# Gated attention and channel mix on one core: state products between half-chunks accumulated in the output's PSUM bank, merged scans, and the low parts of four weights formed by TensorE

## The chip, the cores and the metric

The kernel runs on one core of a Trainium2 chip. The metric is device time in microseconds (us) of one execution. The median of three runs of the kernel before is 344.0 us (342.59 to 344.41).

## What is computed

For 4 batches, 8 heads, 768 positions and a head size of 48, a gated linear attention runs over the positions; its output, 384 features for each position, goes through a channel mix with a shift by one position, 1024 hidden features and a sigmoid gate. All is float32.

```python
for t in range(S):
    state = alpha[:, :, t, :, None] * state + einsum('bhd,bhe->bhde', k[:, :, t], v[:, :, t])
    y[:, :, t] = einsum('bhd,bhde->bhe', q[:, :, t], state)
# x = y, heads joined to 384 features; x_prev = x shifted by one position
xk = mu_k * x + (1 - mu_k) * x_prev
xr = mu_r * x + (1 - mu_r) * x_prev
k = maximum(xk @ w_k, 0)
out = sigmoid(xr @ w_r) * ((k * k) @ w_v)
```

## The kernel before

**Attention.** The sequence of each batch is cut into three segments of 256 positions (12 segments, numbered `a`), each of two chunks of 128 positions (24 chunks, numbered `i`), each of two half-chunks of 64. For a segment, VectorE (DVE) runs scans over `alpha`: `forth` (L380) makes running products, three scans of 256 columns, one for each feature tile; `turn` (L417) takes reciprocals of their last columns; `back` (L424) makes the products from the other end, three scans of 255 columns. `times` (L408) multiplies q and k by them. GpSimd (POOL) copies end values aside (`ends`, L396 and L398), and transfers move the rows of the fourth head pair (`gather`, L446).

For a chunk, TensorE (PE) transposes k (`trans`, L483), ScalarE (ACT) copies that out (`keep`, L661). `update` (L500) multiplies k and v into the state's growth of both half-chunks; it lies in the PSUM tile `yu` beside the output. `scores` (L512) multiplies k and q into the PSUM tile `sp`; DVE applies the mask (`masked`, L597) and adds the growth to the state (`advance`, L628, L631, at a segment's end L633). `intra` (L528) multiplies masked scores and v into `yu`; `inter(i, 0)` (L550) adds the products of q with the state to `yu`, for the heads whose rows of the array go with that bank; `inter(i, 1)` makes the products for the other half, which would be written from rows 0 to 63 into the bank of rows 64 to 127 and the other way round, and writes them into free columns of `sp`. ACT copies the output from `yu` (`leave`, L575), and `crossed` (L585) adds the products in `sp` to it, two DVE additions for a chunk. `spread` (L594) moves rows of the output by two transfers and `prefix` (L568, L570) on POOL fills the column of the position before; then the segment is ready for the channel mix.

An attention step on PE is either an `enter` (update and scores of one chunk), a `visit` (intra and inter of one chunk) or, from chunk 4 on (`JOINED`), a visit that also enters the next chunk.

**Channel mix.** The segments go through in seven groups, the first two of one segment (256 columns), the others of two (512 columns). Products are made in three terms, high by high, low by high and high by low part: `mix_ops` blends x (L802, L805) and splits it (L808, L811); `up_ops` (L822 to L837) makes eight tiles of 128 hidden features, squares and splits them; `gate_ops` (L847, L852) makes the gate; `down_ops` (L859) the output, closed by DVE (L981) and stored (L986). The three PSUM tiles `pm` are taken in turn.

**Weights.** They come in ten blocks (`wk` 4, `wr` 2, `wv` 4), through two raw buffers (`RAWS`): load (L751), `head_bits` on ACT (L756), `join` on DVE (L764), the high part on ACT (L772), the low part on DVE by a subtraction (L776). A raw buffer is free for the next block when its low part is made.

**Order.** All jobs are put into a plan with the engine and what each needs. The list `ORDER` fixes the order on each engine; `follow` only sorts the issue across engines by planned start. Each engine's queue, POOL's and SP's (transfers) among them, then runs in order. Ahead of the first channel-mix products, while PE has gaps, zero matmuls fill them (L1074), until the third user of the `pm` tiles has started (`filled`).

Of the kernel before, what the change touches and what calls it, by code (L numbers as in the profile page):

```python
# [33 lines left out]
LMAX = 2 * C  # L34
WMAX = 2 * LMAX
# [17 lines left out]
ISSUE = 0.42  # L53
RAWS = 2
# [11 lines left out]
class Plan:  # L66
# [26 lines left out]
    def rings(self, sizes):  # L93
        for (ring, n), writers in self.first.items():
            for old in self.users.get((ring, n - sizes[ring]), ()):
                for w in writers:
                    if old != w:
                        self.need[w].append(old)
# [15 lines left out]

    def follow(self, sizes, order):

        self.rings(sizes)
        pre, suc = self.links()
        n = len(self.eng)
# [91 lines left out]
def gated_attention_channel_mix(  # L211
# [64 lines left out]
    for t in (none, *rings):  # L276
        POOL.memset(t, 0.0)  # L277
# [979 lines left out]
```

## Time and profile before

| what | value |
|---|---|
| median of three runs | 344.0 us |
| profiled execution, its own time | 343.89 us |
| its span in the trace | 342.2 us |
| PE busy | 325.7 us, 95% of the span |
| DVE busy | 220.4 us, 64% |
| ACT busy | 196.2 us, 57% |
| POOL busy | 17.9 us, 5% |

The profile is of one execution; its own time is 1.7 us more than the span from the first to the last instruction. Busy shares are averages over the whole span; the stretches differ, which the rows below show.

### The profile page before, as it was taken

What the parts mean: (1) busy time and instruction counts of PE and PEld (TensorE: products, weight loads), DVE (VectorE), ACT (ScalarE), POOL (GpSimd) and SP (SyncE); (2) the same over time, 40 slices, a digit from 0 to 9 for tenths busy, and PEclk for the clock granted to TensorE, in tenths of its full rate; (3) what the DMA queues carried; (4) which work ended last, traced back from release to release, by engine and by line L of the source; (5) the groups of instructions that cost most, each with busy time, mean ns of one, the idle gap of its engine ahead of it and who ended that gap; (6) DMA issues with size and microseconds to landing.
All of it is one profiled execution on the core that took longest, in us unless ns stands there. A gap on an engine that the chain in (4) does not pass through costs nothing. (4 is left out here: it accounts for less than half of the span.)

```text
span 342.2 us, 10261 instructions
## 1 busy us (share of the span) xinstructions
PE 325.7 (95%) x4421; PEld 278.7 (81%) x4421; DVE 220.4 (64%) x421; ACT 196.2 (57%) x367; POOL 17.9 (5%) x60
## 2 busy tenths in 40 slices
PE   8868896999999999999999999999999999999992
PEld 8757885999998888888888888888788887888781
DVE  5999998879988949427564896264895112943010
ACT  4548896476664959137742399622498521887100
POOL 7202001000101000000000000000000000000000
PEclk9999999699999999999999999999999999999997
DMA  7988865443453442211163440043510001100011
GB/s 266 326 284 264 284 198 161 121 125 87 119 165 99 96 119 65 79 20 40 18 200 101 150 129 8 2 119 92 149 35 10 0 15 44 61 2 1 1 63 36
DMA packets 17204, 35.54 MB, mean 104 GB/s; under 512 B 3584, under 2 KB 7808, under 8 KB 17152
## 3 DMA queue, kind: packets, MB, share of 16 engines
q1 hardware_dynamic: 17008, 34.81, 34.0%
q8 instruction: 36, 0.59, 0.7%
q14 instruction: 16, 0.13, 0.1%
q10 hardware_dynamic: 144, 0.00, 0.0%
HBM read 26.55 MB, written 4.72 MB: 91 GB/s over the span
## 5 line engine op out<-in xcount | busy, mean ns | idle before, releaser
L822 PE MATMUL pm<-xkh,wkh 128*128 128x512 f32 (+1 forms) x168 | 44.0, 369 | 0.9 <-ACT x L802 0.9
L828 ACT ACTIVATE r<-pm 128x512 f32<-128x512 f32 (+1 forms) x56 | 29.7, 534 | 22.0 <-PE pm L822 21.5
L822 PE MATMUL pm<-xkh,wkl 128*128 128x512 f32 (+1 forms) x168 | 42.2, 359 | 0.0
L822 PE MATMUL pm<-xkl,wkh 128*128 128x512 f32 (+1 forms) x168 | 42.2, 359 | 0.0
L859 PE MATMUL pm<-kha,wvh 128*128 128x512 f32 (+1 forms) x108 | 39.4, 365 | 2.3 <-ACT wvh L772 2.3
L859 PE MATMUL pm<-kb,wvh 128*128 128x512 f32 x120 | 41.3, 401 | 0.0
L859 PE MATMUL pm<-kha,wvl 128*128 128x512 f32 (+1 forms) x108 | 38.3, 355 | 0.7 <-DVE wvl L776 0.7
L859 PE MATMUL pm<-kla,wvh 128*128 128x512 f32 (+1 forms) x108 | 38.2, 353 | 0.0
L822 PEld LDWEIGHTS pm<-xkh,wkl 128*128 128x128 f32 x168 | 29.3, 188 | 6.0 <-issue 1.0
L981 DVE TENSOR_TENSOR sig<-pm,sig 128x512 f32<-128x512 f32 (+1 forms) x21 | 12.7, 611 | 32.1 <-PE pm L859 23.6
L822 PEld LDWEIGHTS pm<-xkl,wkh 128*128 128x128 f32 x168 | 29.3, 188 | 4.9
L802 ACT ACTIVATE x<-xt,mu 128x512 f32<-128x512 f32 (+1 forms) x42 | 25.5, 656 | 12.3 <-DMA xt<-xt 12.1
L822 PEld LDWEIGHTS pm<-xkh,wkh 128*128 128x128 f32 x168 | 28.6, 188 | 4.9
L834 ACT ACTIVATE k<-r 128x512 f32<-128x512 f32 (+1 forms) x56 | 31.5, 565 | 1.0 <-DVE kla L837 0.5
L575 ACT COPY xt<-yu 112x512 f32<-112x512 f32 x24 | 14.0, 584 | 26.6 <-PE yu L550 23.5
L837 DVE TENSOR_TENSOR kb<-k,kb 128x512 fp32r<-128x512 f32 x20 | 13.8, 690 | 20.9 <-ACT k L834 13.8
L805 DVE SCALAR_TENSOR_TENSOR x<-xt,nu,x 128x512 f32<-128x512 f32 (+1 forms) x42 | 27.0, 668 | 0.3 <-ACT x L802 0.3
L859 PEld LDWEIGHTS pm<-kb,wvh 128*128 128x128 f32 x120 | 22.6, 188 | 5.1
L661 ACT COPY ht<-pt 128x384 f32<-128x384 f32 x24 | 16.2, 677 | 16.4 <-PE pt L483 16.3
L859 PEld LDWEIGHTS pm<-kha,wvh 128*128 128x128 f32 x108 | 21.6, 200 | 5.0 <-ACT wvh L772 2.5
L837 DVE TENSOR_TENSOR kla<-k,kha 128x512 fp32r<-128x512 f32 (+1 forms) x36 | 20.0, 566 | 8.3 <-ACT k L834 4.1
L380 DVE TENSOR_TENSOR_SCAN pp<-al,tiny 128x256 f32<-128x256 f32 x36 | 23.5, 679 | 2.4 <-POOL st L277 2.4
(90 smaller groups left out, 614.2 us busy)
## 6 DMA issues: line engine op xcount, KB each, us to landing
v<-v_p SPq DMA_DIRECT2D x12, 400.0 KB, 4.1
al<-al_p SPq DMA_DIRECT2D x12, 384.0 KB, 3.4
q<-q_p SPq DMA_DIRECT2D x12, 384.0 KB, 3.7
k<-k_p SPq DMA_DIRECT2D x12, 384.0 KB, 3.9
out<-sig SPq DMA_DIRECT2D x15, 256.0 KB, 2.1
early<-wk_p SPq DMA_DIRECT2D x4, 768.0 KB, 5.8
early<-wv_p SPq DMA_DIRECT2D x4, 768.0 KB, 5.8
q<-q SPq DMA_DIRECT2D x24, 48.0 KB, 2.7
```

The source lines that it names most:

```text
L380: DVE.tensor_tensor_scan(view(a, pps)[:, p], view(a, als)[:, p], tiny.to_broadcast([128, n]), initial=START, op0=ALU.mult, op1=ALU.max,)
L575: ACT.copy(x[:R].rearrange("r i (s t) -> r i s t", s=2), yu[:R, :, : NP * HC].rearrange("r s (i t) -> r i s t", i=NP),)
L661: ACT.copy(hts[(i + 1) % 2].rearrange("t (r i) -> t i r", i=NT), pt)
L802: ACT.activation(x, now, AF.Copy, scale=mu[:, i, t : t + 1])
L805: DVE.scalar_tensor_tensor(x, prev, nu[:, i, t : t + 1], x, op0=ALU.mult, op1=ALU.add)
L822: PE.matmul(pk, w[:, t, cols], x[:, t], start=part == 0 and t == 0, stop=part == 2 and t == NT - 1,)
L828: ACT.activation(r, pk, AF.Relu)
L834: ACT.activation(k2, r, AF.Square)
L837: DVE.tensor_tensor(lo, k2, hi.bitcast(F32), op=ALU.subtract)
L859: PE.matmul(pv, w[f // 2][:, f % 2, cols], x, start=f == 0 and i == 0, stop=f == NF - 1 and i == 2,)
L981: DVE.tensor_tensor(sig, pv, sig, op=ALU.mult)
```

## The change

- `inter(i, 1)` goes first in a visit and writes into the output tile `yu`; `intra` and `inter(i, 0)` add to it there. Between it and the first product of `intra`, which other rows of the array write into the same bank, stands a signal: a no-operation on POOL that waits for the last product of `inter(i, 1)` and for which the first of `intra` waits. In a joined visit, update and scores of the next chunk lie between. `crossed` and its 48 DVE additions are gone, and `spread` waits for `leave`. The growth moves from `yu` to `sp`.
- Scans: the three tiles of a segment lie behind each other in 771 columns with a separating column before each; one scan of 771 goes over all three, with a tensor `ways` as its second operand that starts each tile anew. Segment 0 keeps three scans of 256 for `forth`, each behind a load of its own. `turn` writes to `ways`; `back` now waits for `ends`. POOL fills the two `ways` tiles at the start.
- The low parts of the four `wk` blocks: for each half of 384 columns one float32 product with the identity and one float32r product with the negated identity into a `pm` tile, and an ACT copy from it. This takes eight turns of `pm` and the third of them is now the one at which the zero matmuls end. The low parts of `wr` and `wv` stay on DVE.
- The first state addition of a batch is an ACT copy (`open`); an `enter` no longer waits for the output of the chunk before.
- The `pm` tiles are dealt in the order in which their users stand in `ORDER`, which is all new.

The new order on PE until the first channel-mix product `up0.0`: trans0, trans1, less k0 (two), enter0, less k1 (two), enter1, trans2, visit0, trans3, visit1, enter2, less k2 and k3 (two each), enter3, visit2, trans4, visit3, trans5, enter4, up0.0. Before, it was: trans0, trans1, enter0, visit0, enter1, trans2, trans3, visit1, enter2, visit2, enter3, up0.0; trans4, trans5, visit3 and enter4 came behind. Between up0.0 and up1.0 the old order has visits 4 and 5 (joined), the new one 4, 5 and 6.

The new order on DVE until the last low part of `xk` of group 0: forth0 (three), turn0, qP0, back0, kP0, join k0, forth1, turn1, qP1, join k1, back1, mask0, state0, kP1, forth2, mask1, state1, join k2, turn2, forth3, join k3, state2, mask2, qP2, back2, two blends, kP2, state3, mask3, one blend, two low parts, join r0, one blend of `xr`, turn3, the last low part. Before, forth3, back2, kP2, state3, mask3 and that blend of `xr` came behind it, and low r0 ahead.

On POOL, the new order has a copy of `ends` or `prefix` between the visit before and the visit in question ahead of 12 of the 19 joined visits (5, 6, 8, 9, 12 to 17, 19 and 21); a visit's no-operation is issued with the visit and stands behind them.

Core of the diff:

```diff
+BY_PE = (('k', 0), ('k', 1), ('k', 2), ('k', 3))
...
+    def turns(self, order, pre, suc, size=3):
+        first = {w[0]: n for (ring, n), w in self.first.items() if ring == "pm"}
+        self.takers = [j for j in order if j in first]
+        self.place = {first[j]: k for k, j in enumerate(self.takers)}
...
+    for t in als:
+        POOL.memset(t[:, ::SEG], 0.0)
+    ways = ring("ways", 2, [128, NT * SEG])
+    for t in ways:
+        POOL.memset(t, FLOOR)
+    POOL.memset(ways[0][:, ::SEG], START)
...
+        if a == 0:
+
+            def piece(p):
+                SP.dma_start(segments(als, a)[:, p, 1:], al_p[:, at + p * n : at + (p + 1) * n])
...
+        def forth():
             DVE.tensor_tensor_scan(
+                whole(pps, a), whole(als, a), ways[0], initial=START, op0=ALU.mult, op1=ALU.max,
+            )
...
         def turn():
-            e = view(a, pps)[:, :np_, n - 1]
-            DVE.reciprocal(e, e)
-
-        rec = add("DVE", 0.17, turn, need=[end, qm], uses=[("pp", a)], name=f"turn{a}")
+            DVE.reciprocal(ways[1][:, LMAX::SEG], whole(pps, a)[:, LMAX::SEG])
+
+        rec = add("DVE", 0.17, turn, need=first, takes=[("ways", a)], uses=[("pp", a)], name=f"turn{a}")
...
+        def back():
             DVE.tensor_tensor_scan(
+                whole(pps, a)[:, ::-1], whole(als, a, 1)[:, ::-1], ways[1][:, ::-1], initial=0.0,
+                op0=ALU.mult, op1=ALU.max,
             )
...
-    grown = yu[:, :, NP * HC : NP * (HC + D)].rearrange("r s (p e) -> r s p e", p=NP)
+    grown = sp[:, :, NP * HC : NP * (HC + D)].rearrange("r s (p e) -> r s p e", p=NP)
...
-                            start=y == 0 and s not in opened, stop=False, skip_group_check=True,
+                            start=False, stop=False, skip_group_check=True,
                         )
+                        if first is None:
+                            first = one
+                            tc.add_manual_dep(
+                                one.ins, told.ins.name, after, reason="row tiles change banks"
+                            )
...
-                if cross:
-                    to = sp[oo, j, (NP + h) * HC : (NP + h + 1) * HC]
-                else:
-                    to = yu[oo, s, y * HC : (y + 1) * HC]
...
+                wide = HB if cross else D
+                last = PE.matmul(
+                    yu[o * HB : o * HB + wide, s, y * HC : (y + 1) * HC],
+                    before[i, s][rr, at : at + wide], q[rr, p, t0 : t0 + HC],
+                    start=bool(cross) and h == 0, stop=not cross, skip_group_check=True,
+                )
...
-    def crossed(i):
-        a, c = CH[i]
-        x = xview(a)[:, :, 1 + c * C : 1 + (c + 1) * C]
-        for s in range(2):
-            part = x[:R, 1 - s :: 2, s * HC : (s + 1) * HC]
-            DVE.tensor_tensor(
-                part, part,
-                sp[:R, 1 - s, NP * HC : (NP + 2) * HC].rearrange("r (a t) -> r a t", a=2),
-                op=ALU.add,
-            )
...
+            def visit(i=i, enter=enter, joined=joined):
+                last = inter(i, 1)
+                told = POOL.nop()
+                tc.add_manual_dep(told.ins, last.ins.name, after, reason="row tiles change banks")
+                if joined:
+                    enter()
+                intra(i, told)
+                inter(i, 0)
...
+            def less(pm=pm, cut=cut):
+                PE.matmul(pm(), ident, w[:, cut], start=True, stop=False)
+                PE.matmul(pm(), minus, h2[:, cut], start=False, stop=True)
+
+            jp = add(
+                "PE", 5 * mm(NT * 128), less, need=[rd], takes=[("pm", k)], uses=[("raw", i)],
+                name=f"less {key}{f}.{n0}",
+            )
+            ends.append(
+                add(
+                    "ACT", act(NT * 128), lambda pm=pm, cut=cut: ACT.copy(l2[:, cut], pm()), need=[jp],
+                    uses=[("pm", k)], name=f"low {key}{f}.{n0}",
+                )
+            )
...
-    filled = set(plan.first["pm", 2])
+    filled = {plan.takers[2]}
```

## Rows read from the trace of the kernel before

**Rows 1.** Busy times in four stretches: stretch, length, then busy us (count) by engine

```profile
core 0: us, PE busy (x) PEld busy (x) DVE busy (x) ACT busy (x) POOL busy (x), PEclk, DMA share, GB/s
0.00:35.20 35.20, 28.97 (x602) 26.68 (x602) 30.44 (x54) 20.61 (x32) 10.87 (x35) 1.00 0.85 284
35.20:58.00 22.80, 19.43 (x365) 18.34 (x357) 20.54 (x43) 19.09 (x44) 1.13 (x2) 1.00 0.70 211
58.00:65.00 7.00, 6.25 (x28) 5.95 (x29) 6.90 (x14) 4.20 (x9) 0.00 (x0) 0.51 0.42 124
65.00:336.20 271.20, 271.08 (x3436) 227.74 (x3435) 161.80 (x314) 152.30 (x283) 5.94 (x23) 1.00 0.26 72
```

**Rows 2.** PE's timeline, 7 to 60 us: start, us, operation [idle before]

```profile
7.88 2.72 PE L1074 MATMUL pm<-zero 112*112 112x112 f32 x26
...
33.92 0.83 PE L500 MATMUL yu<-v,ht 64*64 64x48 f32 x32
...
35.22 0.51 PE L822 MATMUL pm<-xkh,wkh 128*128 128x256 f32 x2
36.63 0.28 PE L822 MATMUL pm<-xkh,wkh 128*128 128x256 f32 x1 [0.91 <-ACT x L802]
...
44.49 0.69 PE L528 MATMUL yu<-am,v 64*64 64x64 f32 x32
...
45.57 0.62 PE L822 MATMUL pm<-xkh,wkh 128*128 128x256 f32 x3
...
58.05 0.48 PE L859 MATMUL pm<-kha,wvh 128*128 128x256 f32 x1 [2.33 <-ACT wvh L772]
59.23 0.58 PE L859 MATMUL pm<-kha,wvl 128*128 128x256 f32 x1 [0.70 <-DVE wvl L776]
```

**Rows 3.** ACT's timeline around 56 us

```profile
56.20 1.06 ACT L756 ACTIVATE tops<-early 128x768 f16<-128x768 bf16 x1 [2.56 <-DMA early<-wv_p]
```

**Rows 4.** DVE's timeline: the first three scans, and group 0's last low parts

```profile
4.46 1.86 DVE L380 TENSOR_TENSOR_SCAN pp<-al,tiny 128x256 f32<-128x256 f32 x3 [2.44 <-POOL st L277]
...
34.85 1.09 DVE L811 TENSOR_TENSOR xkl<-x,xkh 128x256 fp32r<-128x256 f32 x3
```

**Rows 5.** Groups by line and shape: count, busy us, mean ns of one, idle before

```profile
L408 DVE TENSOR_TENSOR k<-k,pp 128x768 f32<-128x768 f32 x12 | 11.4, 954 | 0.2
L776 DVE TENSOR_TENSOR wkl<-early,wkh 128x768 fp32r<-128x768 f32 x4 | 3.8, 943 | 0.0
L597 DVE TENSOR_TENSOR am<-sp,mask 128x512 f32<-128x512 f32 x24 | 16.4, 683 | 5.3 <-PE sp L512 5.3
L661 ACT COPY ht<-pt 128x384 f32<-128x384 f32 x24 | 16.2, 677 | 16.4 <-PE pt L483 16.3
L628 DVE TENSOR_TENSOR st<-st,yu 112x192 f32<-112x192 f32 x24 | 8.4, 348 | 20.8 <-ACT xt L575 19.8 <-PE yu L550 1.0
L585 DVE TENSOR_TENSOR xt<-xt,sp 112x128 f32<-112x128 f32 x48 | 11.5, 281 | 7.8 <-ACT xt L575 5.9 <-PE sp L512 1.8
L417 DVE RECIPROCAL pp<-pp 128x3 f32<-128x3 f32 x12 | 2.1, 175 | 0.9 <-POOL pe L398 0.4
```

**Rows 6.** DMA issues: count, size and median us from issue to landing

```profile
early<-wk_p SPq DMA_DIRECT2D x4, 768.0 KB, 5.8
...
xt<-xt SPq DMA_DIRECT2D x24, 48.0 KB, 2.7
```

**Rows 7.** PE's timeline of one joined visit, from its start to the next product

```profile
104.48 0.77 PE L500 MATMUL yu<-v,ht 64*64 64x48 f32 x29
...
106.67 0.97 PE L822 MATMUL pm<-xkh,wkh 128*128 128x512 f32 x3
```

**Rows 8.** L570 on POOL: semaphore instructions, ns min/median/max

```profile
L570 POOLq EVENT_SEMAPHORE  x14: 17/43/43, 31.2 to 281.8; - x14
```

**Rows 9.** POOL's timeline: two copies behind waits

```profile
15.24 1.70 POOL L396 COPY pends<-pp 128x6 f32<-128x6 f32 x1 [7.56 <-DVE pp L380]
...
31.52 1.88 POOL L570 COPY xt<-xt 128x3 f32<-128x3 f32 x1 [13.94 <-DMA xt<-xt]
```

More of the change, by code (lines that the diff above doesn't have):

```diff
@@ L118, in follow @@
         pre, suc = self.links()
+        self.turns(order, pre, suc)
         n = len(self.eng)
@@ L430, in attention_inputs @@
             add(
-                "DVE", 0.17 + 2.083e-3 * n, lambda p=p: back(p), need=[rec], uses=[("pp", a), ("al", a)],
-                name=f"back{a}.{p}",
+                "DVE", 0.17 + 2.083e-3 * NT * SEG, back, need=[rec, end, qm], uses=[("pp", a), ("al", a), ("ways", a)],
+                name=f"back{a}.0",
             )
-            for p in range(np_)
         ]
@@ L666, in attention_products @@
                 )
-                ready = [tcopy[i + 1], *half_k[a], *half_q[a], *loads[a]["v"]]
+                ready = [ht, *half_k[a], *half_q[a], *loads[a]["v"], last_mask, last_adv]
                 touched = [("ht", i + 1), ("k", a), ("q", a), ("v", a)]
-                opened = (0,) if marks[i + 1] is None else (0, 1)
-            if i >= 0:
-                mine = [("am", i), ("q", CH[i][0]), ("v", CH[i][0]), *before[i]]
-            joined = i >= JOINED and more
-            def visit(i=i, out=i >= 0, more=more, opened=opened if joined else ()):
-                if more and joined_at(i):
-                    update(i + 1, opened)
-                if out:
-                    intra(i, opened)
-                    inter(i, 0)
-                    inter(i, 1)
-                if more and joined_at(i):
-                    scores(i + 1)
@@ L684, in enter @@
-            def enter(i=i, opened=opened):
-                update(i + 1, opened)
-                scores(i + 1)
-            vis = None
-            if i >= 0:
-                need += ready if joined else []
-                vis = add(
-                    "PE", 2.28 if joined else 1.25, visit, need=need,
-                    uses=mine + (touched if joined else []), name=f"visit{i}",
-                )
-                last_visit = vis
-                a, c = CH[i]
+            joined = i >= JOINED and more
@@ new lines, in enter @@
+            def enter(i=i):
+                update(i + 1)
+                scores(i + 1)
+            def visit(i=i, enter=enter, joined=joined):
[6 more added lines that the diff above has]
+                inter(i, 0)
+            if more and not joined:
+                vis = add("PE", 1.4, enter, need=ready, uses=touched, name=f"enter{i + 1}")
@@ L697, in attention_products @@
+            if i >= 0:
+                a, c = CH[i]
+                out = add(
+                    "PE", 2.38 if joined else 1.4, visit,
+                    need=[last_mask, last_adv, last_leave, *half_q[a], *(ready if joined else [])],
+                    uses=[("am", i), ("q", a), ("v", a), *before[i], *(touched if joined else [])],
+                    name=f"visit{i}",
+                )
+                if joined:
+                    vis = out
                 last_leave = add(
-                    "ACT", 0.5, lambda i=i: leave(i), need=[vis], takes=[("xt", slot_of[a])], name=f"leave{i}"
+                    "ACT", 0.5, lambda i=i: leave(i), need=[out], takes=[("xt", slot_of[a])], name=f"leave{i}"
@@ L699, in attention_products @@
                 )
[L700 to L710 removed]
+                done.setdefault(a, []).append(last_leave)
@@ L717, in attention_products @@
                 ending = c == GROUPS[a][2] - 1
+                opening = before[i + 1, 0] is none
+                opens = []
+                if opening:
+                    new = before[i + 1, 1]
+                    opens = [
+                        add(
+                            "ACT", 0.36, lambda new=new: ACT.copy(by_pair(new), grown[:R, 0]), need=[vis],
+                            takes=[("st", x) for x in held[i + 1][:1]], name=f"open{i + 1}",
+                        )
+                    ]
                 last_adv = add(
-                    "DVE", 0.75 + (0.3 if ending and not final(a) else 0.0), lambda i=i: advance(i + 1),
-                    need=[vis, last_adv, *(rescale.get(a, ()) if ending else ())],
+                    "DVE", (0.4 if opening else 0.75) + (0.3 if ending and not final(a) else 0.0), lambda i=i: advance(i + 1),
+                    need=[vis, last_adv, *opens, *(rescale.get(a, ()) if ending else ())],
                     takes=[("st", x) for x in held[i + 1]],
```

173 lines of the change are left out of this document (96 added, 77 removed), and 77 rows, old and new, of the table ORDER.

## Prediction

> **What bounds the kernel now.** I read the busy times by stretch first [rows 1]. From 65.0 to 336.2 us TensorE is busy for 271.08 of 271.20 us, DVE for 161.8 and ACT for 152.3. In that stretch only work taken off PE, or added to it, counts; 11.5 us of DVE additions [rows 5] are worth nothing there. What a faster DVE can give lies before 65 us. Between 35.2 and 58 PE is idle for 22.80 - 19.43 = 3.4 us, between 58 and 65 for another 0.75, and there its granted clock is 0.51, the lower of its two levels (1.2 GHz). PE's timeline names the waits [rows 2]: 0.91 us for ACT at 36.63, 2.33 for ACT's `wvh` at 58.05, 0.70 for DVE's `wvl` at 59.23. The second goes back to a transfer, for which ACT sat 2.56 us before `tops` at 56.20 [rows 3]: two raw buffers, freed by the low parts on DVE. After that wait the clock is at half until about 65, so some 5.7 us from 59.23 did the work of 2.9. Lost after the first product at 35.2: 3.4 + 0.75 + 2.9 = 7.0 us.
>
> Ahead of 35.2 DVE sets the pace. It starts scanning at 4.46 and makes the last low parts of group 0 until 34.85 + 1.09 = 35.94 [rows 4], busy for 30.44 of 35.2 us [rows 1]. PE's 28.97 us there hold zero matmuls, 26 of them in one row [rows 2]; PE has room.
>
> So the end is: start of the first product (U), the PE work still to do, the waits of PE (W), and what the visits cost more (V). Before: 35.2 + 293.9 + 7.0 = 336.1, with the last product and the store after it up to 342.2 untouched.
>
> **DVE until the first product.** Both orders stand in the section on the change. Gone: four low parts at 0.94, six additions of `crossed` at 0.28, one state addition at 0.35 [rows 5], and low r0 (0.94) goes behind: 6.7. Four merged scans: three of 256 take 1.86 [rows 4]; merging three leaves the columns and saves at most two fixed parts, and an instruction on three columns takes 0.175 [rows 5], so 0 to 0.35 each. I take 0.3, nearer the bound that the instruction shows: 1.2. New ahead of it: two more merged scans (at most 1.86 less 0.3, and some 0.2 more for the backward one: 3.3), kP2 0.95, state3 1.0 (three at 0.35), mask3 0.68 [rows 5], a blend at 0.4 and turn3 0.17: 6.5. Net -1.4, rounded to -1.2 since these means overlap a little; bounds -2 and 0. The first load in three pieces may start DVE up to 0.9 earlier, but POOL's fills of `ways` (two of 771 columns) delay `ends`, for which `back` now waits: taken together 0, bounds -1 and +1.
>
> A hold comes in. Load k3 needs the raw buffer that `less k1` frees, and that needs high k1 on ACT behind join k1: by DVE's list join k1 ends at about 15, less k1 at about 17.5. The load takes 5.8 [rows 6], so `top` ends at 17.5 + 5.8 + 1.1 [rows 3] = 24.4. `leave1` stands behind it in ACT's queue (to 25.0), then two `spread` issues of 1.3 in all and 2.7 to land [rows 6]: 29.0, scale 29.5. DVE's list wants the blend at 28.3 and a second one right after, whose scale stands behind three ACT copies of low parts. I take 2.0 us; bounds 0 (ACT catches up) and 4.
>
> U = 35.9 - 1.2 + 2.0 = 36.7, bounds 34.5 and 39. So the first product itself comes no earlier. SP's two extra issues push k0 and wk0 by about 0.9, but join k0 now stands behind kP0, which covers it.
>
> **PE until then.** Eight `less` jobs: float32 products come as two records (16 products of `update` give 32 [rows 2]); at 2.72 us for 26 records of 112 columns, 384 columns take 2 x 0.36 = 0.72, the float32r one 0.24 (512 columns: 0.97 for three [rows 7]). Eight times 0.96 = 7.7 us, in place of zero matmuls: nothing, while PE has that room; if not, up to 7.7 on U. ACT gets eight copies like `ht`'s, 0.68 [rows 5] = 5.4 us, and has 35.2 - 20.6 = 14.6 free there [rows 1], though in order: part of the hold above.
>
> What the order does win: visit3 (44.49 to 45.57, 1.08) and enter4 (33.92 to 35.22, 1.3) now lie ahead of U, in PE's gaps [rows 2]. Two transposes besides are not counted. Left behind U: 293.9 - 2.4 = 291.5.
>
> **Waits after U.** With three segments prepared instead of two, the attention no longer runs behind. But the jobs up to the first product of group 1 come, by these rows, to about 28 us on each of PE, DVE and ACT. low v1 frees the buffer for wv3 at about 49.7; 5.8 to land, 1.1 for `top`, join 0.95 and two low parts 1.9 make 59.5, while PE gets to the products that need them at about 57. I take W = 3, bounds 1 and 7 (as now).
>
> **The visits.** A joined visit takes 106.67 - 104.48 = 2.19 us [rows 7] and holds the same products after the change. The signal goes PE to POOL to PE; a semaphore instruction on POOL takes 0.04 us [rows 8], a copy in its way up to 1.9 [rows 9]. Update and scores, 1.3 us [rows 2], lie between and cover it: 0 to 0.1 for each of 19. The four unjoined visits before U wait openly, in PE's gaps; the last one too, for about 0.2. V = 0.6, bounds 0 and 2.
>
> **Sum.** 36.7 + 291.5 + 3 + 0.6 = 331.8, against 336.1: 4.3 us less. The profiled execution took 343.9, 0.1 under the median, so 339.6.
>
> **The clock.** PE's clock fell once, after the 2.33 us of idle time at 55.7 [rows 1, 2], and never while zero matmuls filled the gaps. They now end with the third `pm` user, `less k1`, at about 16 instead of 36 us, and gaps of 1 to 2 us between attention steps stay. The Trainium skill, "TensorE: Matmul & The Clock Gate", section "HAM oscillation", says that waits between bursts of matmuls take the clock back to half rate, and by it visit3, enter4 and the first products would run at half. The trace agrees for the fall at 58 us; no row shows sparse work without fill. In the sum I keep the full clock, because the `less` jobs are dense work.
>
> **Rivals.**
> - More than forecast: DVE's list goes through without the hold and the wv loads come in time. U 35.5, W 1, V 0.3: 328.3, so 336.1. For it: DVE has no `crossed` in the way; against it: three full queues.
> - The gain goes back into PE's waits: half clock ahead of the first products (as the one stretch lost 2.9), or the wv blocks late again with the clock after them. W = 7: 343.6, no change. For it: the same two raw buffers, and the end of the fill.
> - Slower, by POOL's queue. A copy of `ends` or `prefix` stands ahead of 12 joined visits. Both wait, the one for a scan, the other for a transfer, and then take up to 1.7 and 1.9 us [rows 9]; whatever goes beyond the 1.3 us of cover stops PE in its full stretch. At 0.75 us for each of 12 it is 9 us: 348.6. It decides from 6.0 / 12 = 0.5 us each. Against it: most copies come long after their scan, and later ones may be short; the order leaves some microseconds between most pairs.
>
> **Chances.** Forecast 0.48, more 0.20, gain given back 0.20, POOL's queue 0.12. A measurement of this kernel can tell about 0.5% (1.7 us) from no change. Faster by more: 0.48 + 0.20 and a little of the third, 0.69; same 0.18; slower 0.13. The range goes from below the better case, 335.0, to above the third, 345.5; left out are most of POOL's case and a U at its lower bound.
>
> **What would show it.** Right: the first L822 product (its new line) at 36 to 38 us with visit3 and enter4 before it; one wait of 1 to 3 us for the wv blocks near 57; PE full from there; no wait of `intra` for POOL over 0.2 us. The hold shows as DVE idle before the first blend, with ACT's `top` waiting for its load. Wrong: a granted clock of 0.5 between 25 and 40 us, first products after 39, or PE idle before `intra` in the full stretch.

## The result, and the profile after

The kernel after takes 346.8 us (median of 19 runs, 344.9 to 350.2), the kernel before 343.0 (19 runs, 342.1 to 345.2): ratio 1.0107, 95% interval 1.0085 to 1.0128. The longest execution, 350.2, is a slow one and is left out of the ratio. The kernel after is slower by 3.7 us, where 4.3 us less were forecast. The profiled execution has a span of 344.8 us against 342.2.

The stretches of the kernel after, with the columns of [rows 1]:

```profile
0.00:35.20 35.20, 27.96 (x420) 22.79 (x421) 26.31 (x32) 19.63 (x34) 9.72 (x37) 0.85 0.77 243
35.20:58.00 22.80, 18.48 (x441) 16.44 (x441) 17.95 (x33) 17.38 (x39) 0.83 (x4) 0.93 0.72 229
58.00:65.00 7.00, 7.00 (x169) 6.75 (x169) 5.90 (x12) 5.86 (x15) 3.39 (x4) 1.00 0.87 283
65.00:336.20 271.20, 270.97 (x3335) 228.76 (x3335) 151.31 (x244) 156.91 (x295) 6.96 (x19) 1.00 0.25 72
```

From 58 us on PE is full, as before from 65. The wait for `wvh` and the half clock behind it are gone. What was lost lies ahead of 58 us. DVE was busy for 4.1 us less until 35.2 (26.31 against 30.44), and idle for so much longer; PE's clock was 0.85 there, before 1.00.

PE's timeline (start, us, operation, idle time before), against [rows 2]; L895 is the channel mix's first product, L839 the first half of a `less` job, L553 the first of an `enter`, L608 of a visit:

```profile
25.38 0.46 PE L608 MATMUL yu<-q,st 48*64 48x64 f32 x16 [0.30 <-issue]
...
28.47 1.18 PE L553 MATMUL sp<-v,ht 64*64 64x48 f32 x30 [1.03 <-DMA v<-v_p]
...
30.61 1.65 PE L839 MATMUL pm<-early,ident 128*128 128x384 f32 x2
...
35.01 0.94 PE L839 MATMUL pm<-early,ident 128*128 128x384 f32 x2 [0.49 <-ACT wkl L848]
...
36.06 0.79 PE L553 MATMUL sp<-v,ht 64*64 64x48 f32 x30
...
37.16 0.44 PE L608 MATMUL yu<-q,st 48*64 48x64 f32 x16
...
39.75 0.46 PE L608 MATMUL yu<-q,st 48*64 48x64 f32 x16 [0.61 <-ACT xt L635]
40.44 0.69 PE L584 MATMUL yu<-am,v 64*64 64x64 f32 x31 [0.23 <-POOLq L721]
42.32 0.21 PE L584 MATMUL yu<-am,v 64*64 64x64 f32 x1 [1.19 <-issue]
...
43.17 0.97 PE L553 MATMUL sp<-v,ht 64*64 64x48 f32 x30
...
45.03 1.01 PE L895 MATMUL pm<-xkh,wkh 128*128 128x256 f32 x3
...
51.22 0.46 PE L608 MATMUL yu<-q,st 48*64 48x64 f32 x16
...
53.38 0.55 PE L536 MATMUL pt<-ident,k 128*128 128x128 f32 x3
...
57.38 0.38 PE L895 MATMUL pm<-xkh,wkh 128*128 128x256 f32 x1 [2.16 <-issue]
...
338.20 0.40 PE L932 MATMUL pm<-kb,wvh 128*128 128x512 f32 x1
```

Five things are to be seen. The first product comes at 45.03, before at 35.22. Ahead of it stand visit3 (39.75) and enter4 (43.17). enter2 comes at 28.47, where the kernel before had it at 27.91 (its row stands below). Four `less` jobs, from 30.61 to 36.06, stand between enter2 and enter3, and visit2 starts behind them at 37.16, before at 31.67. And twice PE stops in the middle of a job with nothing open ("issue"), for 1.19 and 2.16 us; with a third stop of 0.30 us ahead of visit1 that is 3.65 us. The kernel before has no such stop over 0.2 us. The joined visit, 51.22 to 53.38, takes 2.16 us against 2.19 [rows 7].

DVE's timeline from join k3 to the last low part of `xk` (L884):

```profile
28.30 0.96 DVE L815 SCALAR_TENSOR_TENSOR early<-early,tops 128x768 uint32<-128x768 uint32 x1 [1.65 <-ACT tops L807]
30.75 0.35 DVE L678 TENSOR_TENSOR st<-st,sp 112x192 f32<-112x192 f32 x1 [1.49 <-PE sp L565]
...
33.06 1.76 DVE L477 TENSOR_TENSOR_SCAN pp<-al,ways 128x771 f32<-128x771 f32 x1
35.77 0.88 DVE L878 SCALAR_TENSOR_TENSOR x<-xt,nu,x 128x256 f32<-128x256 f32 x2 [0.95 <-ACT x L875]
...
38.49 0.69 DVE L646 TENSOR_TENSOR am<-sp,mask 128x512 f32<-128x512 f32 x1
...
41.51 0.40 DVE L884 TENSOR_TENSOR xkl<-x,xkh 128x256 fp32r<-128x256 f32 x1
```

DVE waits 1.65 us for `top` k3 and 1.49 for enter2. State2 then starts at 30.75, in the kernel before at 30.28. From there to the end of the last low part it is 11.2 us, before 5.7.

ACT's timeline: `top` k3, a copy of a low part (L848), the first scale of group 0 (L875) and the copy of visit2's output (L635):

```profile
27.21 1.06 ACT L807 ACTIVATE tops<-early 128x768 f16<-128x768 bf16 x1 [1.35 <-DMA early<-wk_p]
...
33.70 0.48 ACT L848 CAST wkl<-pm 128x384 fp32r<-128x384 f32 x1 [2.45 <-PE pm L840]
34.07 0.51 ACT L875 ACTIVATE x<-xt,mu 128x256 f32<-128x256 f32 x1
...
39.14 0.56 ACT L635 COPY xt<-yu 112x512 f32<-112x512 f32 x1
```

And four milestones of the kernel before, PE's enter2 and visit2 and the two parts of its first product:

```profile
27.91 0.79 PE L500 MATMUL yu<-v,ht 64*64 64x48 f32 x30
...
31.67 0.69 PE L528 MATMUL yu<-am,v 64*64 64x64 f32 x32 [1.23 <-DVE am L597]
...
35.22 0.51 PE L822 MATMUL pm<-xkh,wkh 128*128 128x256 f32 x2
36.63 0.28 PE L822 MATMUL pm<-xkh,wkh 128*128 128x256 f32 x1 [0.91 <-ACT x L802]
```

### The profile page after: what moved, and what is told of

Its sections match the earlier page's. It is cut to its first block, busy times and chain, and to the rows that moved or that the text cites. A ratio compares the mean times of both kernels' runs of the same rounds, so it can differ in the third digit from the quotient of the medians.

```text
span 344.8 us, 10099 instructions
## 1 busy us (share of the span) xinstructions
PE 326.8 (95%) x4369; PEld 276.3 (80%) x4369; DVE 202.2 (59%) x320; ACT 199.8 (58%) x380; POOL 20.9 (6%) x63
## 5 line engine op out<-in xcount | busy, mean ns | idle before, releaser
L895 PE MATMUL pm<-xkh,wkh 128*128 128x512 f32 (+1 forms) x168 | 44.5, 372 | 2.2 <-issue 2.2
L895 PE MATMUL pm<-xkh,wkl 128*128 128x512 f32 (+1 forms) x168 | 42.5, 362 | 0.0
L895 PE MATMUL pm<-xkl,wkh 128*128 128x512 f32 (+1 forms) x168 | 42.3, 360 | 0.0
L932 PE MATMUL pm<-kha,wvh 128*128 128x512 f32 (+1 forms) x108 | 38.2, 354 | 0.0
L932 PE MATMUL pm<-kha,wvl 128*128 128x512 f32 (+1 forms) x108 | 37.0, 342 | 0.0
L932 PE MATMUL pm<-kla,wvh 128*128 128x512 f32 (+1 forms) x108 | 37.0, 342 | 0.0
L1049 DVE TENSOR_TENSOR sig<-pm,sig 128x512 f32<-128x512 f32 (+1 forms) x21 | 12.8, 610 | 37.3 <-PE pm L932 32.5
L895 PEld LDWEIGHTS pm<-xkh,wkh 128*128 128x128 f32 x168 | 28.8, 190 | 7.0 <-issue 2.4
L895 PEld LDWEIGHTS pm<-xkh,wkl 128*128 128x128 f32 x168 | 29.6, 190 | 5.1
L910 DVE TENSOR_TENSOR kla<-k,kha 128x512 fp32r<-128x512 f32 (+1 forms) x36 | 20.3, 568 | 22.6 <-ACT kha L904 16.1
L895 PEld LDWEIGHTS pm<-xkl,wkh 128*128 128x128 f32 x168 | 29.5, 189 | 4.9
L875 ACT ACTIVATE x<-xt,mu 128x512 f32<-128x512 f32 (+1 forms) x42 | 26.6, 661 | 10.4 <-DVE xkl L884 5.8
L635 ACT COPY xt<-yu 112x512 f32<-112x512 f32 x24 | 14.0, 582 | 26.7 <-PE yu L608 26.7
L646 DVE TENSOR_TENSOR am<-sp,mask 128x512 f32<-128x512 f32 x24 | 16.4, 684 | 12.9 <-PE sp L565 11.7
L932 PE MATMUL pm<-kb,wvl 128*128 128x512 f32 x60 | 23.7, 395 | 0.0
```

Of the source, the lines that this page charges most:

```text
L635: ACT.copy(x[:R].rearrange("r i (s t) -> r i s t", s=2), yu[:R, :, : NP * HC].rearrange("r s (i t) -> r i s t", i=NP),)
L646: DVE.tensor_tensor(ams[i % 2], sp[:, :, : NP * HC].rearrange("c j (p t) -> c j p t", p=NP), mask.unsqueeze(1).unsqueeze(1).to_broadcast([ ...
L875: ACT.activation(x, now, AF.Copy, scale=mu[:, i, t : t + 1])
L895: PE.matmul(pk, w[:, t, cols], x[:, t], start=part == 0 and t == 0, stop=part == 2 and t == NT - 1,)
L910: DVE.tensor_tensor(lo, k2, hi.bitcast(F32), op=ALU.subtract)
L932: PE.matmul(pv, w[f // 2][:, f % 2, cols], x, start=f == 0 and i == 0, stop=f == NF - 1 and i == 2,)
```

## The experiments

Each kernel computes the whole result. The table gives the median, the ratio to the kernel before on the same chip with its 95% interval, and from one profiled execution the start of the first channel-mix product, the start of PE's last product, and the sum of PE's stops over 0.2 us which no dependency explains. The kernels were timed on different chips, so microseconds of two rows compare only roughly; their ratios compare better.

| kernel | us | ratio | first product | last product | stops |
|---|---|---|---|---|---|
| before | 343.0 | 1 | 35.2 | 335.7 | 0 |
| after | 346.8 | 1.0107 (1.0085 to 1.0128) | 45.0 | 338.2 | 3.7 |
| 1 all parts, old order | 349.6 | 1.0214 (1.0152 to 1.0276) | 39.2 | 340.3 | 0 |
| 2 low parts on DVE | 344.5 | 1.0050 (1.0025 to 1.0075) | 43.5 | 335.6 | 1.7 |
| 3 transfers reordered | 345.9 | 1.0085 (1.0056 to 1.0114) | 43.6 | 335.9 | 2.1 |
| 4 fill goes on | 348.2 | 1.0138 (1.0085 to 1.0192) | 47.4 | 341.1 | 0 |
| 5 old order, no low parts on PE | 346.8 | 1.0104 (1.0056 to 1.0152) | 37.5 | 338.8 | 0.3 |
| 6 crossed products and opening copy, old order | 346.4 | 1.0089 (1.0050 to 1.0128) | 37.3 | 338.0 | 0 |
| 7 attention behind the first product | 349.2 | 1.0179 (1.0131 to 1.0226) | 36.9 | 339.7 | 1.7 |
| 8 the same, transfers reordered | 350.2 | 1.0206 (1.0157 to 1.0256) | 38.2 | 341.8 | 2.1 |
| 9 crossed in joined visits only | 345.7 | 1.0059 (1.0026 to 1.0092) | 39.1 | 339.8 | 0 |
| 10 opening copy on DVE | 346.5 | 1.0119 (1.0049 to 1.0190) | 36.7 | 337.4 | 0.8 |
| 11 attention behind, second order | 356.8 | 1.0365 (1.0280 to 1.0449) | 38.5 | 347.7 | 1.8 |
| 12 = 9 with 10 | 344.1 | 1.0051 (1.0018 to 1.0084) | 36.0 | 336.7 | 0.4 |
| 13 new order with 2, 9 and 10 | 350.2 | 1.0212 (1.0159 to 1.0265) | 48.0 | 343.4 | 7.1 |
| 14 = 12 with more fill | 347.6 | 1.0129 (1.0113 to 1.0145) | 38.7 | 340.4 | 3.0 |
| 15 before with more fill | 344.4 | 1.0051 (1.0030 to 1.0071) | 35.8 | 335.6 | 0.6 |
| 16 = 2 with more fill | 348.2 | 1.0143 (1.0098 to 1.0187) | 45.0 | 339.6 | 1.9 |
| 17 stream shifted by 16 products | 344.6 | 1.0040 (1.0017 to 1.0063) | 44.4 | 338.6 | 2.1 |
| 18 stream shifted by 32 products | 344.4 | 1.0028 (1.0002 to 1.0054) | 42.9 | 334.6 | 0.6 |

One profile is one execution, and its stops need not be those of the timed runs. No kernel beats the one before.

### First round: parts, transfers and fill (1 to 4)

Kernel 1 keeps every part and takes the old order by names; where a job was split or merged, the new ones stand in its place. Kernels 2 to 4 keep the new order. Where an edit changes an order, the lines below tell it by the names of the jobs; in the kernels it is a list of numbers.

```diff
 kernel 1
-ORDER = new order
+ORDER = old order; less k0 to k3 and their ACT copies where low k0 to k3 stood
 kernel 2
-BY_PE = (('k', 0), ('k', 1), ('k', 2), ('k', 3))
+BY_PE = ()
 kernel 3, SP's first 21 jobs
-al0.1 q0 al0.0 al0.2 k0 wk0 al1 wk1 q1 v0 gat q0 gat k0 k1 al2 gat pe0 wk2 gat q1 al3 wk3 v1 gat k1
+al0.1 q0 al0.0 al0.2 wk0 k0 al1 wk1 gat q0 q1 v0 gat k0 k1 v1 al2 wk2 gat pe0 gat q1 wk3 al3 gat k1
 kernel 4, zero matmuls into a free slot of pt
-    filled = {plan.takers[2]}
+    filled = {plan.takers[10]}
 ...
```

Kernel 1: 

> All parts of the change, but every job that both kernels have stands where the old order had it; the products that form low parts stand where the old order had the subtraction, each copy behind its product. Theory 1 (the new order is what costs: it puts eight low-part products, loads and attention steps ahead of the first channel-mix product, which comes at 45.0 us instead of 35.2): first product at 34 to 38 us, and the time at or below the kernel before, 337 to 343 us. Rival (the parts themselves cost, wherever they stand: low-part products in TensorE's queue, the fills at the start): first product after 40 us and a time of 345 to 350.

Kernel 2: 

> The changed kernel, with the low parts of the wk blocks subtracted by DVE again (0.94 us each, where the last product of each block stood in the order); by that the zero matmuls go on until the third channel-mix product. Theory 2 (the low-part products in TensorE's queue cost: enter3 stood behind four of them until 36.06 although its inputs were there at 32.0, partly at half clock): first product 4 to 7 us earlier than 45.0, and 339 to 343 us. Rival (transfers that land late set it: block k2 and k3 and v1): first product at 43 or later, 345 to 348.

Kernel 3: 

> The changed kernel, with the first 21 jobs of SP's queue in another order: wk0 ahead of k0, the gather of q0 ahead of q1 and v0, v1 ahead of al2, al3 behind wk3. Theory 3 (late transfers cost: v1, issued at 20.65 and awaited by enter2 until 28.47, and the gathers behind early loads): enter2 at 24 to 26, first product 3 to 5 us earlier than 45.0, 341 to 344 us. By theory 2: enter2 earlier, but the low-part products wait for the same blocks and the first product moves by under 1.5 us: 345 to 348.

Kernel 4: 

> The changed kernel, with the zero matmuls going on until the third channel-mix product, into a free quarter of the transposes' tile instead of a product tile. Theory 4 (the lower clock between 10 and 46 us costs; by the trace 0.75, 0.61 and 0.71 in three stretches of 5 us): clock at 1.0 until 50 us, first product 2 to 4 us earlier, 342 to 345 us. Rival (TensorE waits there anyway, and the clock costs nothing, or the zero matmuls stand in the way): within 1 us of the changed kernel or slower.

Kernel 1 has its first product 4 us later than before in the same order, and its wv products wait again (3.44 and 0.60 us). So the new order alone is not the cause; the parts themselves cost time. Kernel 2 wins 1.5 us on the first product and 2.3 in time. In kernel 3 two gathers of k land in 5.5 us instead of 7.2 and v1 is loaded earlier. enter2 does not wait for it any more and begins at 27.33, right behind visit1 and 1.1 us earlier than in the kernel after, but a stop falls into it:

```profile
27.33 0.23 PE L553 MATMUL sp<-v,ht 64*64 64x48 f32 x1
28.39 0.73 PE L553 MATMUL sp<-v,ht 64*64 64x48 f32 x29 [0.83 <-issue]
```

So the transfers are worth some 1 us at enter2, not the 2.5 to 4.5 expected, and how much of that would reach the end was not shown. Kernel 4 loses: PE's clock is 0.50 in 30 to 35 us all the same, and the zero matmuls wait for `pt`'s copies, 3.8 us in all.

### Which part costs in the old order (5, 6, 9, 10, 12)

Kernel 5 is kernel 1 with `BY_PE = ()`. Kernel 6 also takes back the merged scans and the load in pieces. Kernel 9 is kernel 6, but visits 0 to 3, which are not joined, keep the old way (products aside, now in free columns of `yu`, and DVE's additions). Kernel 10 is kernel 6 with the opening copy on DVE. Kernel 12 is 9 and 10 together.

```diff
 kernels 9 and 12
+                if i < JOINED:
+                    intra(i)
+                    inter(i, 0)
+                    inter(i, 1, True)
+                    return
 ...
 kernels 10 and 12
-                            "ACT", 0.36, lambda new=new: ACT.copy(by_pair(new), grown[:R, 0]), need=[vis],
+                            "DVE", 0.36, lambda new=new: DVE.tensor_copy(by_pair(new), grown[:R, 0]), need=[vis],
```

Kernel 5: 

> All parts but the low parts on TensorE (VectorE makes all low parts again), in the order of before. With all parts the old order had its first channel-mix product at 39.2 us, before it was at 35.2. If the low parts on TensorE cost that (eight jobs on PE, eight copies in ACT's queue): first product at 34.5 to 36, wv waits below 3 us in all, 340 to 343. Rival, that the merged scans and the start (GpSimd's fills ahead of the first load) cost it: first product still at 38 to 39.5, 345 to 348.

Kernel 6: 

> Only the crossed products in the output's bank with the signal through GpSimd, and the opening copy on ACT: separate scans, one load, low parts on VectorE, the order of before without the 48 additions. If the visits cost nothing more: first product at 34.5 to 35.2 (VectorE loses six additions of 0.28 us ahead of it), end minus first product 299 to 301 as before (300.9), 341.5 to 343, ratio 0.995 to 1.000. Rival, that the signal itself costs in the old order: four unjoined visits with an open wait put the first product at 36 or later and end minus first product over 302, ratio over 1.003.

Kernel 9: 

> As the kernel with the crossed products alone (346.4 us, first product 37.3), but visits 0 to 3, which no update and scores cover, keep the old way: products aside, then VectorE's additions. Theory: an unjoined visit that waits openly for the signal is longer by about 0.45 us, ACT's copy after it ends 1.1 us later (27.8 instead of 26.7), and top k3 and join k3 stand behind that copy. Then: visit1's copy back at 26.7 to 27.2, first product at 35 to 36, 342.5 to 344. Rival, that the joined visits or the opening copy cost the 3.4 us: first product still at 37 or the end minus first product over 302, 345.5 to 347.

Kernel 10: 

> As the kernel with the crossed products alone (346.4 us, first product 37.3), but the opening copy of a batch's state is made by VectorE. Theory (unjoined visits' open signal): no gain, first product 36.8 to 37.6, 345.5 to 347. Rival (the opening copy waits in ACT's queue: VectorE was idle 0.77 us for it at 18.8): first product at 36.5 or earlier, 344 to 345.5.

Kernel 12: 

> Old order, separate scans, low parts on VectorE; crossed products in the output's bank in joined visits alone, and the opening copy of a batch on VectorE. With the crossed products everywhere visit1's copy ended 1.1 us late; with the opening copy on ACT visit0 began 0.6 to 1.9 us late, as the copy stands behind top k2 in ACT's queue. If these two are what the crossed part costs: visit0 at 18.0 to 18.6, first product at 35 to 36, 342.3 to 344.3, ratio within 0.998 to 1.003. Rival, that the joined visits or the new place of the growth cost it: 345 or more, ratio over 1.005.

In the old order the crossed products, with the opening copy on ACT, cost 3.4 us; the forecast had the visits at 0.6 and nothing for the copy. PE's timeline of kernel 6 at visit1 and at the first product (L868):

```profile
26.00 0.46 PE L581 MATMUL yu<-q,st 48*64 48x64 f32 x16
26.69 0.69 PE L557 MATMUL yu<-am,v 64*64 64x64 f32 x32 [0.23 <-POOLq L694]
27.18 0.43 PE L581 MATMUL yu<-q,st 48*48 48x64 f32 x16
...
37.29 0.62 PE L868 MATMUL pm<-xkh,wkh 128*128 128x256 f32 x3 [1.81 <-ACT x L848]
...
38.62 0.84 PE L868 MATMUL pm<-xkh,wkh 128*128 128x256 f32 x3
```

And ACT's of kernel 6, the copy after visit1 and `top` r0 behind it (the expectation for kernel 9 calls it `top` k3, but k3 is the block before it, at 25.31):

```profile
27.78 0.59 ACT L608 COPY xt<-yu 112x512 f32<-112x512 f32 x1 [1.39 <-PE yu L581]
28.27 1.08 ACT L780 ACTIVATE early<-early 128x768 f16<-128x768 bf16 x1
```

The same two in the kernel before:

```profile
26.69 0.59 ACT L575 COPY xt<-yu 112x512 f32<-112x512 f32 x1 [0.64 <-ACT tops L756]
27.41 1.10 ACT L756 ACTIVATE early<-early 128x768 f16<-128x768 bf16 x1
```

Visit1 waits openly for the signal and takes about 1.6 us to 27.6; before, it began 0.34 us earlier and took 1.15. ACT's copy ends 1.1 us later, and `top` r0, which stands behind it in ACT's queue, starts 0.86 later. DVE then waits 1.02 us for it, and state2 behind that starts at 31.12 instead of 30.28. The first product waits 1.81 us, PE's clock falls to its lower level (0.84 us for three products of 256 columns instead of 0.52), and the wv products wait later.

Kernels 9 and 10 alone were no clear gain. In the profile of 9 the opening copy stood behind `top` k2 in ACT's queue and visit0 began at 20.32 instead of 18.26; that of 10 had half clock in visit1. With both, in kernel 12, 10 of 11 runs lie below all six of kernel 6: 2.3 of the 3.4 us are gone by the medians, by the ratios 0.4 of 0.9%, with intervals that overlap. So these two make a part of it. The ratio that is left, 1.0051, lies outside what was expected (up to 1.003) and where the rival begins (over 1.005); whether the joined visits, the clock (0.50 from 26 to 32 us in its profile) or the place of the instruction stream makes it, no run tells. Kernel 5, with the merged scans besides, went in time as its rival had it, with no gain (346.8 against 346.4); its first product, 37.5, lies between what the theory and the rival had.

### Is it the order of the work (7, 8, 11, 13)

Kernel 7 is kernel 2 with other orders after state2. Kernel 8 adds kernel 3's transfers. Kernel 11 moves kP3 and ht6 forward. Kernel 13 is kernel 2 with the visits and the opening copy of kernel 12.

```diff
 kernels 7, 8, 11, on PE
-trans4 visit3 trans5 enter4 up0.0 to up0.4 visit4+enter5 trans6 up0.5 to up0.7
+up0.0 to up0.4 trans4 visit3 trans5 enter4 up0.5 up0.6 visit4+enter5 trans6 up0.7
 on DVE, after state2
-mask2 qP2 back2 two blends kP2 state3 mask3 blend two low parts join r0 ... low part
+mask2 qP2 three blends three low parts back2 kP2 rest0.0 state3 mask3 ...
 kernel 11 besides
+kP3 ahead of the low parts of wr; ht6 ahead of the tops of wv on ACT
```

Kernel 7: 

> Kernel with low parts on VectorE (first product 43.5 us, end minus first product 292.5), but after state2 VectorE takes group 0's blends and low parts first and back2, kP2, state3 and mask3 after them, and trans4, visit3, trans5 and enter4 go behind five products of group 0. Theory, the work put ahead of the first product makes it late: first product at 36 to 38 (spread of segment 0 lands at about 33.4, then three scales, blends and low parts), end minus first product 294 to 297, so 338.5 to 342. Rival, transfers and clock set it: first product at 41 or later whatever stands behind state2, over 343.

Kernel 8: 

> The same with SP's first 21 jobs in the order that took the gathers from 7.0 to 5.1 us. By the theory that the work ahead sets the first product, no more than 0.5 us against the kernel it is compared with; by the rival that transfers do, 1 to 2 us earlier.

Kernel 11: 

> As the kernel with the attention behind the first products (first product 36.9, then full until 53, then 2.35 and 3.21 us of waits for kP3 and for ht6, which stood behind tops of wv in ACT's queue), with kP3 ahead of the low parts of wr on VectorE and ht6 ahead of the tops of wv on ACT. If what an early first product gives is only lost to those two orders: waits after 50 us below 2.5 in all, last product at 333 to 336, 339 to 343. Rival, that the work up to group 1 is as long on the three engines whatever stands first: other waits of 4 us or more take their place (wv products near 60 to 66 us), 344 to 349.

Kernel 13: 

> The new order with the low parts on VectorE (344.5 us, first product 43.5, waits behind it small), the unjoined visits in the old way and the opening copy on VectorE. If these two cost time here as in the old order: first product at 41.5 to 43, last product at 333.5 to 335, 341 to 343.5. Rival, that in this order the transfers set enter2 and they cost nothing: first product 43 to 44, 344 to 345.5.

PE's timeline of kernel 7, its first product and its two longest waits:

```profile
36.94 0.81 PE L895 MATMUL pm<-xkh,wkh 128*128 128x256 f32 x3
...
53.97 0.90 PE L536 MATMUL pt<-ident,k 128*128 128x128 f32 x3 [2.35 <-DVE k L464]
...
60.01 0.90 PE L536 MATMUL pt<-ident,k 128*128 128x128 f32 x3 [3.21 <-ACT ht L705]
```

The first half of the theory holds: without visit3 and enter4 ahead of it on PE, and back2, kP2, state3 and mask3 on DVE, the first product comes at 36.9, 6.5 us earlier than in kernel 2. Kernel 8 is no better for its transfers. The second half falls: the time is 4.7 us worse than kernel 2's, and both profiles have one stop of 1.7 us at the same place, in visit1. The attention now runs late, and kP3 (2.35 us) and `ht` (3.21) are waited for at 52 to 60 us, at half clock. Kernel 11 was to mend that and made it worse (behind the first product 2.9 us of waits for DVE's k, 4.5 for the state and 2.2 for a low part of `xr`). An early first product is no gain by itself; it says only which work was put ahead. Kernel 13 missed as well: its profile has 7.1 us of stops.

### Clock and fill (14 to 16)

```diff
-FILL = 0.6
+FILL = 0.85
```

Kernel 14: 

> As the kernel with the crossed products in joined visits alone and the opening copy on VectorE (344.1 us, ratio 1.005; its clock was 0.50 from 26 to 32 us after 1.13 us of idle time at 22.6), but with 0.85 of each planned gap filled by zero matmuls instead of 0.6. Theory, the half clock in the attention steps is what is left of the cost: clock 1.00 from 16 us on, first product 0.6 to 1 us earlier (35.2 to 36), 342 to 343.5. Rival, the zero matmuls now push attention steps back by as much, or the rest is elsewhere: 344 to 346.

Kernel 15: 

> The kernel before with the same fill of 0.85; its clock was at full ahead of the first product with 0.6. Nothing to win there: 342.5 to 344. If the fill delays attention steps: 345 or more, and then the run beside it has to be read against that.

Kernel 16: 

> New order with low parts on VectorE (344.5 us, first product 43.5; its clock was 0.50 from 27 to 35 us, after a stop of 1.66 us in the middle of visit1 which no dependency explains), with the fill of 0.85. If the half clock there comes from idle gaps: clock at full, first product at 42 to 43, 342 to 344. If it comes from the stop in visit1: half clock there again and 344 to 346.

The zero matmuls held the clock at 1.00 to 32 us in kernel 14, and it became slower: 347.6. The control, kernel 15, lost 1.4 us with the fill, and its profile has a stop of 0.56 us. Kernel 16 had the clock at 0.81 instead of 0.62 in 26 to 35 us and lost 3.7. And kernel 14's profile shows two stops which kernel 12's did not, 1.12 us up to 30.4 and 1.92 us up to 36.6, with about half clock (0.57) from 38 to 42 behind the second. That put the stops in question: more zero matmuls are also more instructions.

### The instruction stream (17, 18)

The DMA table of the profile has a queue of kind "instruction" with 36 packets of 16 KB over the span; no row says whose instructions they are. In the kernel after one of them lies in 39.75 to 40.0, ahead of the stop that begins at 41.1, and one in 54.50 to 54.75, ahead of the one that begins at 55.2. The row of that quarter of a microsecond (queue, kind: packets, MB, share):

```profile
q8 instruction: 1, 0.02, 30.0%
```

Most packets go by without a stop, so this alone shows nothing. Kernels 17 and 18 are the kernel after with 16 and 32 products of one column at the very start, where PE waits; the first `trans` stays at 11.7 to 11.8 us.

```diff
+    for i in range(16):
+        PE.matmul(pms[0][:1, :1], zero[:, :1], zero[:, :1], start=True, stop=True)
```

Kernel 17: 

> The changed kernel (346.8 us; its PE stopped for 1.19 us up to 42.32, in visit3, and for 2.16 us up to 57.38, in a product of group 0, with no dependency open and an instruction load of PE's queue beginning 1.4 and 0.7 us before) with 16 products of one column more at the very start, where PE waits for the first trans. Nothing else moves. If PE's instruction loads make the stops: they stand 64 instructions earlier in the work, so at other places or not at all, and the time moves by what they take, to 343.5 to 346 or 348 to 350. Rival, the stops belong to those places of the work: same places within 0.5 us and 346 to 347.6.

Kernel 18: 

> The same with 32 such products (128 instructions). If instruction loads make the stops: other places again, and a time that differs from the changed kernel's or from the run with 16 by 1 us or more. Rival: same places, 346 to 347.6.

PE's timeline of kernel 18 from enter2 to the first product (L897), and its last product:

```profile
27.79 0.97 PE L555 MATMUL sp<-v,ht 64*64 64x48 f32 x30 [1.67 <-DMA v<-v_p]
...
39.09 0.46 PE L610 MATMUL yu<-q,st 48*64 48x64 f32 x16 [0.40 <-ACT xt L637]
...
41.60 0.79 PE L555 MATMUL sp<-v,ht 64*64 64x48 f32 x30 [0.43 <-DMA v<-v_p]
...
42.88 0.62 PE L897 MATMUL pm<-xkh,wkh 128*128 128x256 f32 x3
...
334.56 0.40 PE L934 MATMUL pm<-kb,wvh 128*128 128x512 f32 x1
```

Two rows of kernel 17's, the stop ahead of visit1 and its longest:

```profile
25.56 0.46 PE L610 MATMUL yu<-q,st 48*64 48x64 f32 x16 [0.28 <-issue]
...
53.87 0.27 PE L586 MATMUL yu<-am,v 64*64 64x64 f32 x1 [1.44 <-issue]
```

No job changed its place in a queue, and the time fell by 2.1 and 2.4 us (by the ratios 2.3 and 2.7); neither interval touches that of the kernel after. The long stops stand elsewhere (kernel 17: 1.44 us up to 53.87) or are gone (kernel 18 has 0.25 at 66.2). The short one ahead of visit1, 0.28 to 0.30 us, stays at its place of the work in all three. The span of kernel 18's profile is 3.7 us shorter than that of the kernel after, whose stops made 3.65. So for the long stops it went as the theory had it, and the rival (same places, 346 to 347.6) is out. Two reserves: the extra products also keep PE busier until 10 us, and the clock in 10 to 15 us was 0.75 in the kernel after, 0.95 and 1.00 in these. In kernel 18's profile enter2 comes 0.7 us earlier than in the kernel after, ahead of the long stops, so that much of its gain need not be theirs; in kernel 17's it comes 1.2 us later. Between 25 and 35 us the clock fell in all three. And the profile of kernel 17 is of its longest execution (347.0 us), that of kernel 18 of a short one (343.0). What a stop is was not shown, only that the long ones move with the stream.

This bounds what the other runs can say. Every edit above changes PE's stream too, so a difference of some 2 us between two of these kernels is no proof of its edit by itself. The 2.3 and 2.7 us of the low parts (2 against the kernel after, 1 against 5; 0.6 and 1.1% by the ratios) are near that size, and stay open. That kernel 5 equals kernel 6 is subject to the same.

## Why the prediction was wrong, step by step

- **The sum.** Forecast for the end of the last product 331.8, in the profile 338.6 (338.20 + 0.40): 6.8 us too low. U is 8.3 of it, the work and waits behind U give 1.5 back. Against the kernel before, the first product comes 9.8 us later and what stands behind it is 7.3 us shorter (293.6 against 300.9), so the last product ends 2.5 us later.
- **U, the step that failed.** "So the first product itself comes no earlier": 36.7, bounds 34.5 to 39; measured 45.0, and 42.9 in kernel 18, whose stops ahead of it come to 0.3 us instead of 1.5. Laid on the hold of 2.0 us alone (bounds 0 and 4), that would be a hold of 10.3 and 8.2. Four things in that step were wrong.
  - "What the order does win: visit3 and enter4 now lie ahead of U, in PE's gaps", costed at nothing. They are no gap work. Visit3 needs mask3, which DVE ended at 39.2, and waited 0.61 us for ACT's copy of visit2's output, which ended at 39.7; enter4 stands behind visit3 and trans5. From visit3's start to the first product are 5.3 us, 3.8 in kernel 18. Kernel 7, which puts both behind the first product and four jobs of DVE with them, shows the size of the whole: 6.5 us.
  - The eight `less` jobs, "in place of zero matmuls: nothing, while PE has that room". Behind enter2 it had none: from 28.47 to 39.14 PE was busy for 10.04 of 10.67 us, four `less` jobs took it from 30.61 to 36.06, and visit2 came 5.5 us later than before. This is a part of U and not the larger one: kernel 2, without these jobs on PE, has visit2 at 34.83 and the first product only 1.5 us earlier.
  - The net of -1.2 us on DVE set work removed ahead of state2 against work added behind it as if they were one heap. enter2 was at 27.91 before and 28.47 after, where it waits 1.03 us for `v1`. What DVE won ahead of that point became idle time. What was added behind it (back2, kP2, state3, mask3: 4.5 us) counted in full in DVE's stretch from state2 to the last low part, 11.2 us instead of 5.7.
  - `top` k3 was to end at 24.4; it started at 27.21. Its load was issued at 20.3 instead of 17.5, and DVE waited 1.65 us for it. So the hold was seen rightly, as DVE's wait for `top`, and was too small: the scale that was to follow at 29.5 started at 34.07, on ACT behind a copy of a low part for which ACT had waited 2.45 us.
- **Merged scans.** 0.3 us each was assumed; a forward scan of 771 columns takes 1.74 to 1.76 us against 1.86 for three of 256 [rows 4], so 0.1; a backward one takes 1.76 against 2.03 for three of 255 (the kernel before, at 7.92), so 0.3.
- **The unjoined visits**, "wait openly, in PE's gaps": in the old order this and the opening copy, which the forecast did not cost, made a part of 3.4 us, by way of ACT's queue. What they cost in the new order no run separates (kernel 13's profile has 7.1 us of stops).
- **The clock.** The sum kept full clock, "because the `less` jobs are dense work". The granted clock was 0.75 in 10 to 15 us, 0.61 in 25 to 30, 0.71 in 30 to 35, 0.82 in 40 to 45 and 0.84 in 45 to 50, the lower level for a part of each. It fell in 25 to 30 us behind idle times of 0.99, 0.30 and 1.03 us, and in 40 to 45 behind the stop of 1.19 us. Of the four `less` jobs after enter2 the first and a part of the second ran slowly in it (1.65 us in the row at 30.61, 0.84 for the third job's). By what the forecast took from the Trainium skill, "TensorE: Matmul & The Clock Gate", section "HAM oscillation", visit3, enter4 and the first products were to run at half rate; the trace agrees for enter4 and the first product, which stand behind the stop, and not for visit3, as the clock was 1.00 from 35 to 40 us.
- **The work behind U and V: right; W: too high.** 291.5 + 3 + 0.6 = 295.1 forecast, 338.6 - 45.0 = 293.6 measured, with a stop of 2.16 inside it; 292.1 in kernel 18. W = 3, bounds 1 and 7, came as 0 in the kernel after and as 0.6 and 1.3 in kernels 18 and 17. That the wv blocks came in time is no proof of the reckoning, as the first product came 8.3 us later than in it. Behind U one visit waits for the signal, for 0.2 us.
- **The rivals.** POOL's queue was false: a `prefix` copy took 2.98 us at 57.77, and no visit waited for it. "The gain goes back" was the nearest, but named the waits behind U; the loss lay ahead of it.
- **What no rival had.** The stops: by the ratios 2.3 and 2.7 of the 3.7 us go when the stream is shifted, with the reserves told there. What is then left, 0.40% and 0.28% (1.4 and 1.0 us), is the nearest that these runs come to what the change as such costs; the lower end of the second's interval lies just above no change, and both kernels still have stops in their profiles (2.1 and 0.6 us). The stream of the kernel before, which has no stop, was not shifted in this way. Kernel 15, which is that kernel with more zero matmuls, has a stop of 0.56 us, so its place may be a lucky one.

## What to carry to other kernels

Work taken off an engine counts up to the next thing that this engine waits for and no further; sum the removed and added work separately for each stretch between such points. A job moved "into a gap" of another engine is free only if its inputs are ready in that gap, so put it on the chain and look at what it waits for. And before a difference of half a per cent is put down to an edit, shift the instruction stream by a few products that do nothing and time that too.

## What was not expected of the hardware

PE stopped for 0.3 to 3.2 us, mostly in the middle of jobs, without any open dependency, in most of the changed kernels and only ahead of 75 us; 16 or 32 products of one column at the start moved the long stops and took 2.1 to 2.4 us off the time. A clock that falls after a stop makes it dearer (kernel 14: 1.92 us, then 4 us at 0.57). And filling PE's gaps more densely gave kernel 14 a clock of 1.00 until 32 us and yet made it slower than kernel 12; the kernel before, whose clock was 1.00 there anyway, lost 1.4 us by it. Denser fill also shifts the stream, so how much of this is the fill's own was not shown.
